# A gated-loop attention with a SwiGLU layer: the norm's sums spread by a tile of ones, and a power on 128 columns

## The chip, the cores and the metric

The kernel runs on one core of one Trainium2 chip. The core has five engines that work side by side, each through its own list of instructions in order: TensorE (PE in the profile, with its weight loads as PEld), VectorE (DVE), ScalarE (ACT), GpSimd (POOL) and SyncE (SP, which only issues DMA transfers here). The metric is the device time of one execution in microseconds, the median of several runs. Everything is in fp32. SBUF is the on-chip memory, PSUM the memory that PE writes its products to, in eight banks.

## What is computed

Cut to its core, the reference is this:

```python
# attention: batch 4, heads 8, 768 steps, head size 48
mag = np.sqrt(a_re**2 + a_im**2)
scale = np.minimum(mag, 0.999) / (mag + 1e-6)
for t in range(S):                       # S_re, S_im: (B, H, 48, 48)
    S = (a_t * scale_t) * S + k_t v_t^T  # complex gate, row by row
    y[:, :, t] = q_t @ S.real
x = y.transpose(0, 2, 1, 3).reshape(3072, 384)
# feed-forward: 384 -> 1536 -> 384
rms = np.sqrt(np.mean(x * x, axis=-1, keepdims=True) + 1e-6)
xn = x / rms * rms_g
g = xn @ w_gate
out = (g / (1 + np.exp(-g)) * (xn @ w_val)) @ w_out
```

The change touches the line of `rms` and the division by it.

## The kernel before

**Tiles.** The 3072 tokens are 24 chunks of 128 (C = 128), six to a batch. A chunk's attention output stands transposed in PSUM, `yT`: 128 features on the partitions, 3 blocks of features (ND = 3) by 128 tokens along the columns. So a token is a column, and its sum of squares runs over the partitions and the three blocks.

**Stages.** For each chunk `attend(n)` makes the masked scores, the output `yT` and the next state; its last part, with the stage name "norm", makes the normalized `xT`. Two chunks are a group (`GROUPS`, L670), and after the second of them `feed(g, xT)` multiplies the group's 256 columns of `xT` with the gate and value weights (groups `bank<-xT,wg` and `bank<-xT,wv` in the profile), takes silu and product into `hT`, and multiplies with `wo`; from the third group on (`split`) the last product is done with seven half products and sums on DVE (tiles `mid`, `ot`, `S` views of `hT`). Ahead of the chunks, `gates(u)` works on the complex gates of one or two chunks (tiles `t`, `in`, `turns`, `kin`, `rot`), on ACT and DVE, and moves `rot` to `kq` by DMA.

**The norm, step by step (L1123 to L1149).**
1. ACT squares `yT` into `sq`; DVE multiplies `yT` by the weights `gcol` into `yg` and adds the three blocks of `sq` into the first. For the first four chunks (`LIGHT` units) ACT makes `yg` instead and PE adds the blocks.
2. PE: `sq` is loaded as weights and multiplied with the single column `ones` (L1136, group `bank<-ones,sq`). The result is one column, `col`: a token's sum on each partition.
3. DVE (L1138, helper `ts`): times 1/384, plus 1e-6, into the chunk's column of `ssv`, a tile that keeps these values of all 24 chunks.
4. POOL (L1139): that column to the power -0.5, in `rs`, with a tile `mhalf` of -0.5 as exponent. There are two `rs` tiles, used in turn.
5. PE (L1142, group `bank<-ident,rs`): `rs`, its one column read 128 times, is loaded as weights and multiplied with the identity. The result `wide` has each token's factor on all partitions, along the columns.
6. DVE (L1149, helper `tt`): `yg` times `wide`, spread over the three blocks, into the group's `xT`. `yg` stands in SBUF, `wide` in PSUM.

Both products and `wide` and `col` use bank 7, which the transposes of `kt` use as well. There is one `sq` tile and two of `yg` and `rs`.

**The guard.** At the end the kernel compares kept values with limits in a tile `ok` (L1269 on), adds up the outcomes, and runs a general version if one is out of bounds; it does not run here. One comparison is that `ssv` is at least twice 1e-6.

**What sets the order.** Every operation is recorded by `Flow.add` (L519) with its engine, a cost given by hand, and what it reads and writes; `Flow.schedule` (L550) then plays the list through with these costs and takes, on each engine, of the operations that are ready the one with the earliest due time, worked backwards from the products of the feed. `Flow.issue` (L645) writes the instructions down in that order. So the order is fixed when the kernel is built, by costs and not by what happens on the chip; every instruction's line in the profile is L648, and the groups are told apart by their tiles. A changed cost or operation can move all instructions behind it. DMA transfers are issued on SP in this order too (up to eight outstanding in the planner's account), the weights' on POOL.

Of the kernel before, what the change touches and what calls it, by code (L numbers as in the profile page):

```python
# [14 lines left out]
ALU = mybir.AluOpType  # L15
# [3 lines left out]
P = 128  # L19
C = 128  # L20
# [3 lines left out]
EPS_RMS = 1e-6  # L24
# [437 lines left out]
class Flow:  # L462
# [56 lines left out]
    def add(self, eng, calls, dur, reads=(), writes=(), table=None, land=None, due=None, after=(), behind=()):  # L519
        op = dict(i=len(self.ops), eng=eng, calls=calls, dur=dur, deps=set(), table=table, land=land,  # L520
                  base=due, stage=self.stage, behind={o["i"] for o in behind})
        self.ops.append(op)
        op["deps"].update(o["i"] for o in after)
        for ap in reads:
            self.note(op, ap, False)
        for ap in writes:
            self.note(op, ap, True)
        return op
# [122 lines left out]
def fast(tc, ctx, qT, kT, v, a_re, a_im, w_gate, w_val, w_out, rms_g, out, H, bad):  # L651
# [27 lines left out]
    def room(name, shape, dtype=FP32):  # L679
        t = mem.tile(shape, dtype, name=name, tag=name)  # L680
        row = 1
        for x in shape[1:]:
            row *= x
        rooms[t.tensor.name] = (name, row * mybir.dt.size(dtype))
        keep.append(t)
        return t
# [25 lines left out]
    def tt(o, x, y, op=ALU.mult, eng="DVE", **kw):  # L712
        e = nc.vector if eng == "DVE" else nc.gpsimd
        dur = 0.15 + 1.04e-3 * cols(o) if eng == "DVE" else 0.25 + 2.2e-3 * cols(o)
        return add(eng, [(e.tensor_tensor, (), dict(out=o, in0=x, in1=y, op=op))], dur, [x, y], [o], **kw)
# [7 lines left out]
    def ts(o, x, c1, c2, op0, op1=None, **kw):  # L723
        k = dict(op1=op1) if op1 is not None else {}
        return add("DVE", [(nc.vector.tensor_scalar, (),
                            dict(out=o, in0=x, scalar1=c1, scalar2=c2, op0=op0, **k))],
                   0.15 + 0.52e-3 * cols(o), aps(x, c1, c2), [o], **kw)
# [51 lines left out]
    def mms(list_, dur, **kw):  # L779
        calls, reads, writes = [], [], []  # L780
        for o, l, r, start, stop in list_:
            calls.append((nc.tensor.matmul, (o,), dict(lhsT=l, rhs=r, start=start, stop=stop)))
            reads += [l, r]
            writes.append(o)
        return add("PE", calls, dur, reads, writes, **kw)

    def mm_time(n, m=P):
        return 2 * max(0.84e-3 * n, 0.83e-3 * m)
# [6 lines left out]
    ident = room("ident", [P, P])  # L795
    causal = room("causal", [C, C])
    mhalf = room("mhalf", [P, 1])
    ones = room("ones", [P, 1])
    halfpi = room("halfpi", [P, 1])
    mid = room("mid", [P, 1])  # L800
# [26 lines left out]
    states = [room(f"state{i}", [D2, NP, 2, 80]) for i in range(2)]  # L827
    sqs = [room(f"sq{i}", [P, ND, C]) for i in range(1)]
    ygs = [room(f"yg{i}", [P, ND, C]) for i in range(2)]
    ssv = room("ssv", [P, N])  # L830
    rss = [room(f"rs{i}", [P, 1]) for i in range(2)]
    sgs = [room(f"sg{i}", [P, 512]) for i in range(2)]
    ots = [room(f"ot{i}", [C, DM]) for i in range(2)]
    sums = room("sums", [P, 2, HD * DH])
# [6 lines left out]
    fill(warm, 1.0, due=-300.0)  # L841
    act(warm, warm, AF.Abs_reciprocal_sqrt, due=-300.0)
    for t, x in ((ones, 1.0), (halfpi, PI / 2), (mid, -(RE_MAX + RE_MIN) / 2),
                 (width, -(RE_MAX - RE_MIN) / 2), (mhalf, -0.5), (zeros, 0.0)):
        fill(t, x)
    for t in ves + states:
        fill(t[:, :, :, D:], 0.0)
# [221 lines left out]
    def attend(n):  # L1069
        flow.stage = "attend", n  # L1070
        ve, am, kq = ves[n % 3], ams[n % 2], kqs[n % 2]
        vv = ve[:, :, :, 0:D].rearrange("t m e d -> t (m e) d")
        dma(vv, v[n * C:(n + 1) * C, :].rearrange("t (h d) -> t h d", d=D), behind=moved[min(n - 1, HOLD)] if n else ())
        k, q = kq[:, :, 0:C], kq[:, :, C:2 * C]
        for a in range(2):
            ps = banks[4 + a]
            s = ps.rearrange("s (h t) -> s h t", h=HH)
            mms([(s[:, h], k[:, a * HH + h], q[:, a * HH + h], True, True) for h in range(HH)],
                HH * mm_time(C), due=EARLY.get(n))
            tt(am[:, a * HH:(a + 1) * HH], s, causal.unsqueeze(1).to_broadcast([C, HH, C]))  # L1080
        first, last = n % NCH == 0, n % NCH == NCH - 1
        prev, new = states[(n + 1) % 2], states[n % 2]
        ps = banks[6]
        yT = ps[:, 0:DM].rearrange("p (j t) -> p j t", j=ND)
        lines = [[] for _ in range(4)]
        vf, sf = (x.rearrange("p m e d -> p m (e d)") for x in (ve, prev))
        for i in range(4 * ND):
            j, c = divmod(i, 4)
            m, r = divmod(i, 3)
            o = yT[c * BLK:(c + 1) * BLK, j]  # L1090
            part = [(2 * m, 0)] if r == 0 else [(2 * m, 1), (2 * m + 1, 2)] if r == 1 else [(2 * m + 1, 3)]
            todo = []
            for h, g in part:
                todo.append((vf[:, m, g * BLK:(g + 1) * BLK], am[:, h]))
                if not first:
                    todo.append((sf[:, m, g * BLK:(g + 1) * BLK], q[:, h]))
            for x, (l_, r_) in enumerate(todo):
                lines[c].append((o, l_, r_, x == 0, x == len(todo) - 1))
        order = [lines[c][i] for i in range(len(lines[0])) for c in range(4)]
        mms(order, len(order) * mm_time(C) / 4 * 1.1 + 0.15)  # L1100
        if not last:
            kt = kts[0]
            for a in range(2):
                ps = banks[7 - 3 * a]
                kp = ps[:, 0:HH * D2].rearrange("t (h d) -> t h d", h=HH)
                calls = [(nc.tensor.transpose, (kp[:, h], k[:, a * HH + h], ident[0:D2, 0:D2]), {})
                         for h in range(HH)]
                add("PE", calls, HH * 0.085, [k[:, a * HH:(a + 1) * HH], ident], [kp])
                act(kt[:, a * HH:(a + 1) * HH], kp, AF.Copy)
            ps = banks[5][0:D2, 0:DM]  # L1110
            st = ps.rearrange("p (h d) -> p h d", h=H)
            mms([(st[:, h], kt[:, h], vv[:, h], True, True) for h in range(H)], H * mm_time(D, D2))
            st4 = ps.rearrange("p (m e d) -> p m e d", m=NP, e=2)
            u, i = unit_of[n], n - UNITS[unit_of[n]][0]
            decay = decays[way_of(u)][:, :, i].rearrange("p (m e) -> p m e", e=2).unsqueeze(3).to_broadcast([D2, NP, 2, D])
            new4 = new[:, :, :, 0:D]
            if first:
                tt(new4, st4, decay)
            else:
                tt(new4, st4, prev[:, :, :, 0:D], ALU.add)  # L1120
                tt(new4, new4, decay)

        flow.stage = "norm", n  # L1123
        sq, yg = sqs[0], ygs[n % 2]
        act(sq, yT, AF.Square)
        if unit_of[n] in LIGHT:
            for j in range(ND):
                act(yg[:, j], yT[:, j], AF.Copy, scale=gcol[:, j:j + 1])
        else:
            tt(yg, yT, gcol.unsqueeze(2).to_broadcast([P, ND, C]))  # L1130
            tt(sq[:, 0], sq[:, 0], sq[:, 1], ALU.add)
            tt(sq[:, 0], sq[:, 0], sq[:, 2], ALU.add)
        ps = banks[7]
        col = ps[:, C:C + 1]
        parts = range(ND if unit_of[n] in LIGHT else 1)
        mms([(col, sq[:, j], ones, j == 0, j == parts[-1]) for j in parts], 0.25 * len(parts))  # L1136
        sv = ssv[:, n:n + 1]
        ts(sv, col, 1.0 / DM, EPS_RMS, ALU.mult, ALU.add)  # L1138
        add("POOL", [(nc.gpsimd.tensor_tensor, (), dict(out=rss[n % 2], in0=sv, in1=mhalf,  # L1139
                                                        op=ALU.pow))], 0.9, [sv, mhalf], [rss[n % 2]])  # L1140
        wide = ps[:, 0:C]
        mms([(wide, rss[n % 2].to_broadcast([P, P]), ident, True, True)], 0.25)  # L1142
        g = group_of[n]
        ns = GROUPS[g]
        x, lo = xplace[g]
        wide_ = len(ns) * C
        xT = xTs[x][:, lo:lo + ND * wide_].rearrange("p (j t) -> p j t", j=ND)
        i = n - ns[0]
        tt(xT[:, :, i * C:(i + 1) * C], yg, wide.unsqueeze(1).to_broadcast([P, ND, C]))  # L1149
        return xT  # L1150

    xplace = {g: (g % 3, 0) for g in range(len(GROUPS))}
# [113 lines left out]

    ne = N * ND
    NW = len(looks)
    ok = room("ok", [P, 2 * ne + NU + 2 * NW + N])  # L1269
    okc = room("okc", [P, 1])  # L1270
    ef = ends.rearrange("p j n -> p (j n)")
    o = 0
    for in_, limit, op in ((ef, P_MIN, ALU.is_ge), (ef, 1.0, ALU.is_le), (range_, 0.0, ALU.is_le),
                           (small, 1.25 * 2.0 ** -15, ALU.is_ge), (large, 2.0, ALU.is_lt),
                           (ssv, 2.0 * EPS_RMS, ALU.is_ge)):
        w_ = in_.shape[1]
        ts(ok[:, o:o + w_], in_, limit, None, op)
        o += w_
# [62 lines left out]
```

## Time and profile before

| what | us |
|---|---|
| median of 3 runs | 740.79 (740.71 to 741.93) |
| the profiled execution's own time | 740.29 |
| its span, first to last instruction | 738.6 |
| DVE products `xT<-yg,bank`, 24 in all | 13.1 |
| DVE sums `sq<-sq`, 40 in all | 11.4 |
| PE products `bank<-xT,wg` and `bank<-xT,wv` | 201.0 and 198.4 |

The granted TensorE clock of the execution is 0.987 of full speed. The page gives, for each engine, how long it was busy and what ended its idle time; the chain of work that ended last says which engine's time is the kernel's time. A fp32 product is two instructions on PE, so 24 products are a group of 48. PE's instructions overlap, so what one costs is read from the distance between starts (those of weight loads, PEld, are the clearest), not from its length.

How the guard's and the queues' parts stand in the profile: `ok<-ssv` is one DVE instruction of 179 ns on 128x24, and DMA issues appear on the line SPq of the timeline with the time for which the queue was taken.

### The profile page before, as it was taken

The numbers are of one execution on the slowest core, as the hardware profiler recorded it, in microseconds if no ns is written. First come the engines' busy times: TensorE is split into PE (matmuls) and PEld (weight loads), VectorE is DVE, ScalarE is ACT, GpSimd is POOL, SyncE is SP. The second block draws the span as 40 slices with busy tenths as digits, with TensorE's granted clock in tenths as the row PEclk, the third lists the DMA queues.
The fourth block names the chain that finished last, engine by engine and source line by source line (L and its number), as shares of the span: only waits on it lengthen the run. The fifth ranks groups of instructions, "written<-read, shape, count | busy, mean of one in ns | idle before, by whom it ended". The sixth has DMA issues, their size and how long they took to land.

```text
span 738.6 us, 12320 instructions
## 1 busy us (share of the span) xinstructions
PE 694.7 (94%) x5050; PEld 623.9 (84%) x5050; DVE 470.6 (64%) x738; ACT 332.1 (45%) x450; POOL 39.4 (5%) x71
## 2 busy tenths in 40 slices
PE   0369999999999999999999999999999999999996
PEld 0368877877899899899899899899899899899885
DVE  5989987779987977967646546656834234233121
ACT  8567656937576925813915623722821110110010
POOL 3132100000000000000000000000000000000000
PEclk9968999999999999999999999999999999999999
DMA  8697565536455355535222202314111102200000
GB/s 298 209 294 235 161 154 166 163 82 169 127 138 149 99 154 150 181 106 146 70 65 66 75 12 73 95 27 119 54 40 30 51 12 55 65 1 2 22 0 27
DMA packets 100144, 76.47 MB, mean 104 GB/s; under 512 B 40944, under 2 KB 90864, under 8 KB 100080
## 3 DMA queue, kind: packets, MB, share of 16 engines
q1 hardware_dynamic: 96016, 61.05, 30.3%
q0 software_dynamic: 3264, 14.16, 5.3%
q8 instruction: 42, 0.69, 0.4%
q10 hardware_dynamic: 800, 0.39, 0.2%
q14 instruction: 22, 0.18, 0.1%
HBM read 51.91 MB, written 4.72 MB: 77 GB/s over the span
## 4 chain that ended last, share of the span: by engine, by line
PE 92%; DVE 4%; ACT 1%; POOL 1%; issue 1%; DMA 1%; DVEq 0%; POOLq 0%; ACTq 0%
PE bank L648 92%; DVE wg L648 1%; DVE turns L648 1%; DVE wv L648 1%; DMA in<-in_a_re_dram 1%; ACT t L648 0%; DVE t L648 0%; DVE rot L648 0%; ACT L648 0%; DVE in L648 0%; POOL rs L648 0%; DVE xT L648 0%; ACT turns L648 0%; DVE am L648 0%; ACT wo L648 0%
## 5 line engine op out<-in xcount | busy, mean ns | idle before, releaser
L648 PE MATMUL bank<-xT,wg 128*128 128x256 f32 x864 | 201.0, 383 | 1.9 <-DVE xT L648 1.9
L648 PE MATMUL bank<-xT,wv 128*128 128x256 f32 x864 | 198.4, 379 | 0.0
L648 PEld LDWEIGHTS bank<-xT,wg 128*128 128x128 f32 x864 | 164.8, 192 | 25.1 <-DVE xT L648 2.6
L648 PEld LDWEIGHTS bank<-xT,wv 128*128 128x128 f32 x864 | 163.5, 190 | 22.2
L648 DVE TENSOR_TENSOR hT<-bank,sg 128x512 f32<-128x512 f32 x72 | 49.6, 689 | 120.9 <-PE bank L648 114.9
L648 PE MATMUL bank<-wo,hT 128*128 128x192 f32 (+1 forms) x576 | 123.4, 357 | 0.4 <-DVE hT L648 0.4
L648 PEld LDWEIGHTS bank<-wo,hT 128*128 128x128 f32 x576 | 94.4, 190 | 11.8 <-issue 1.4
L648 ACT ACTIVATE sg<-bank 128x512 f32<-128x512 f32 x72 | 43.0, 597 | 130.4 <-PE bank L648 127.4
L648 ACT ACT_TABLE_LOAD x67 | 86.0, 1283 | 7.3 <-DVE rot L648 4.7
L648 PE MATMUL bank<-kq 96*128 96x128 f32 x384 | 52.3, 290 | 28.2 <-DMA kq<-rot 28.2
L648 PEld LDWEIGHTS bank<-kq 96*128 96x128 f32 x384 | 49.5, 203 | 29.8 <-issue 29.0
L648 ACT ACTIVATE sq<-bank 128x384 f32<-128x384 f32 x24 | 11.8, 491 | 106.7 <-PE bank L648 106.6
L648 DVE TENSOR_TENSOR rot<-kin,turns 128x768 f32<-128x768 f32 x48 | 44.6, 952 | 14.6 <-DMA kq<-rot 14.4
L648 POOL TENSOR_TENSOR rs<-ssv,mhalf 128x1 f32<-128x1 f32 x24 | 19.4, 810 | 586.6 <-DVE ssv L648 498.0
L648 ACT ACTIVATE kt<-bank 128x384 f32<-128x384 f32 x40 | 18.5, 489 | 66.0 <-PE bank L648 65.9
L648 PE MATMUL bank<-sums,hT 128*128 128x192 f32 x240 | 45.1, 329 | 0.0
L648 PEld LDWEIGHTS bank<-sums,hT 128*128 128x128 f32 x240 | 39.4, 190 | 0.0
L648 DVE TENSOR_TENSOR hT<-hT 128x768 f32<-128x768 f32 x40 | 38.2, 955 | 0.9
L648 PE MATMUL bank<-am,ve 128*32 128x128 f32 x768 | 37.8, 281 | 0.0
L648 ACT ACTIVATE turns<-in 128x768 f32<-128x768 f32 (+1 forms) x39 | 29.9, 789 | 17.1 <-DVE rot L648 8.0
L648 DVE TENSOR_TENSOR am<-bank,causal 128x512 f32<-128x512 f32 x48 | 32.7, 686 | 7.1 <-PE bank L648 6.5
L648 ACT ACTIVATE t<-t 128x768 f32<-128x768 f32 (+1 forms) x39 | 30.9, 792 | 7.9 <-DVE t L648 7.2
(108 smaller groups left out, 729.0 us busy)
## 6 DMA issues: line engine op xcount, KB each, us to landing
kq<-rot SPq DMA_DIRECT2D x144, 128.0 KB, 2.4
ve<-in_v_dram SPq DMA_DIRECT2D x24, 192.0 KB, 3.1
kin<-in_q_dram SPq DMA_DIRECT2D x24, 192.0 KB, 2.7
kin<-in_k_dram SPq DMA_DIRECT2D x24, 192.0 KB, 4.1
wo<-in_w_gate_dram SPq DMA_DIRECT2D x6, 768.0 KB, 5.7
out_dram<-ot SPq DMA_DIRECT2D x24, 192.0 KB, 2.2
wo<-in_w_val_dram SPq DMA_DIRECT2D x6, 768.0 KB, 4.3
wo<-in_w_out_dram SPq DMA_DIRECT2D x6, 768.0 KB, 4.3
```

Of the source, the lines that this page charges most:

```text
L648: fn(*args, **kw)
```

## The change

The first product takes a tile of ones, 128x128, as weights and `sq` as the moving side: its result has each token's sum on all partitions, along 128 columns. Scaling (DVE) and power (POOL) are done on 128x128 values instead of 128x1, in place in `rs`, which is 128 columns wide now. The second product is gone, and the product into `xT` reads `rs` in SBUF. `ssv` is gone; instead a DMA puts the first row of `rs` into row n of a tile `most`, filled with ones at the start, and the guard compares `most` with the limit's power. The planner's cost of the power is 1.5 us instead of 0.9; the cost of a product is `mm_time(C)` instead of 0.25. The tile named `mean` is filled with ones; the factor 1/384 stays in the scaling.

```diff
+    mean = room("mean", [P, P])
+    most = room("most", [P, C])
...
-    ssv = room("ssv", [P, N])
-    rss = [room(f"rs{i}", [P, 1]) for i in range(2)]
+    rss = [room(f"rs{i}", [P, C]) for i in range(2)]
...
-                 (width, -(RE_MAX - RE_MIN) / 2), (mhalf, -0.5), (zeros, 0.0)):
+                 (width, -(RE_MAX - RE_MIN) / 2), (mhalf, -0.5), (zeros, 0.0), (mean, 1.0), (most, 1.0)):
...
-        col = ps[:, C:C + 1]
+        wide = ps[:, 0:C]
         parts = range(ND if unit_of[n] in LIGHT else 1)
-        mms([(col, sq[:, j], ones, j == 0, j == parts[-1]) for j in parts], 0.25 * len(parts))
-        sv = ssv[:, n:n + 1]
-        ts(sv, col, 1.0 / DM, EPS_RMS, ALU.mult, ALU.add)
-        add("POOL", [(nc.gpsimd.tensor_tensor, (), dict(out=rss[n % 2], in0=sv, in1=mhalf,
-                                                        op=ALU.pow))], 0.9, [sv, mhalf], [rss[n % 2]])
-        wide = ps[:, 0:C]
-        mms([(wide, rss[n % 2].to_broadcast([P, P]), ident, True, True)], 0.25)
+        mms([(wide, mean, sq[:, j], j == 0, j == parts[-1]) for j in parts], mm_time(C) * len(parts))
+        rs = rss[n % 2]
+        ts(rs, wide, 1.0 / DM, EPS_RMS, ALU.mult, ALU.add)
+        add("POOL", [(nc.gpsimd.tensor_tensor, (), dict(out=rs, in0=rs, in1=mhalf.to_broadcast([P, C]), op=ALU.pow))],
+            1.5, [rs, mhalf], [rs])
+        dma(most[n:n + 1, :], rs[0:1, :])
...
-        tt(xT[:, :, i * C:(i + 1) * C], yg, wide.unsqueeze(1).to_broadcast([P, ND, C]))
+        tt(xT[:, :, i * C:(i + 1) * C], yg, rs.unsqueeze(1).to_broadcast([P, ND, C]))
...
-    ok = room("ok", [P, 2 * ne + NU + 2 * NW + N])
+    ok = room("ok", [P, 2 * ne + NU + 2 * NW + C])
...
-                           (ssv, 2.0 * EPS_RMS, ALU.is_ge)):
+                           (most, (2.0 * EPS_RMS) ** -0.5, ALU.is_le)):
```

## The prediction

> **What bounds the kernel now.** I read the head of the page first: how busy each engine is and who holds the chain of work that ended last.
>
> ```profile
> span 738.6 us, 12320 instructions
> ...
> PE 694.7 (94%) x5050; PEld 623.9 (84%) x5050; DVE 470.6 (64%) x738; ACT 332.1 (45%) x450; POOL 39.4 (5%) x71
> ...
> PE 92%; DVE 4%; ACT 1%; POOL 1%; issue 1%; DMA 1%; DVEq 0%; POOLq 0%; ACTq 0%
> ```
>
> TensorE (PE) holds 92% of the chain, so time that PE loses is time lost. The table of windows, asked for the stretch in which the chain is one run of PE, says whether it has any slack (columns: length, then busy time of PE, PEld, DVE, ACT, POOL, then clock, DMA share and rate):
>
> ```profile
> 117.10:685.00 567.90, 567.90 (x4228) 515.37 (x4228) 359.89 (x579) 249.98 (x327) 14.43 (x20) 1.00 0.32 87
> ```
>
> PE is busy for all of its 567.90 us there. What is taken off PE is a gain; what makes PE wait is a loss; DVE (360 of 568) and POOL (14) have room, so their work counts only where PE waits for its outcome. The groups that the change touches, with shapes kept apart:
>
> ```profile
> L648 POOL TENSOR_TENSOR rs<-ssv,mhalf 128x1 f32<-128x1 f32 x24 | 19.4, 810 | 586.6 <-DVE ssv L648 498.0 <-DVE ends L648 88.6
> ...
> L648 DVE TENSOR_TENSOR xT<-yg,bank 128x384 f32<-128x384 f32 x24 | 13.1, 547 | 6.5 <-PE bank L648 6.5
> ...
> L648 PE MATMUL bank<-ident,rs 128*128 128x128 f32 x48 | 9.9, 289 | 1.8 <-POOL rs L648 1.8
> L648 PE MATMUL bank<-ones,sq 128*128 128x1 f32 x64 | 9.3, 232 | 3.5 <-ACT sq L648 2.9 <-ACT kt L648 0.6
> ...
> L648 DVE TENSOR_SCALAR ssv<-bank 128x1 f32<-128x1 f32 x24 | 3.7, 154 | 9.5 <-PE bank L648 9.5
> ...
> masks.py:199 POOL TENSOR_SCALAR_AFFINE_SELECT ident<-ident 128x128 f32<-128x128 f32 x1 | 0.3, 294 | 0.1
> ```
>
> The power is 24 instructions on one column, and its mean of 810 ns hides two values. Here it is in two places of the timeline (start, length, engine): the first beside a DVE product of two tiles, the second, at 506 us, with DVE idle.
>
> ```profile
> 343.58 0.16 DVE L648 TENSOR_SCALAR ssv<-bank 128x1 f32<-128x1 f32 x1 [0.90 <-PE bank L648]
> 343.65 0.95 DVE L648 TENSOR_TENSOR t<-t,t 128x768 f32<-128x768 f32 x1
> 343.82 1.19 POOL L648 TENSOR_TENSOR rs<-ssv,mhalf 128x1 f32<-128x1 f32 x1 [6.81 <-DVE ssv L648]
> ```
>
> ```profile
> 506.12 0.55 POOL L648 TENSOR_TENSOR rs<-ssv,mhalf 128x1 f32<-128x1 f32 x1 [50.12 <-DVE ssv L648]
> ```
>
> With DVE's product running (it ends at 344.60) the power ends at 345.01, that is 0.41 us after it, and takes 1.19; with DVE idle it takes 0.55. So a power cannot read while DVE reads two tiles of SBUF; of its 0.55, about 0.14 is dispatch and 0.41 the column.
>
> **What the change takes off.** PE loses the 24 second products (48 instructions). One costs PE the distance to the next weight load. The first product of a chunk has the same price, read here: its two loads start at 505.41 and the next at 505.68.
>
> ```profile
> 505.41 0.35 PEld L648 LDWEIGHTS bank<-ones,sq 128*128 128x128 f32 x2
> ...
> 505.68 0.95 PEld L648 LDWEIGHTS bank<-hT 128*128 128x128 f32 x6
> ```
>
> For the second product the same distance is 0.27 (loads at 449.04, next 449.31): 24 x 0.27 = 6.5 us off PE. The first product keeps two weight loads and now streams 128 columns instead of one; scores of 128 columns cost 0.12 per instruction (16 weight loads of bank<-kq in 1.92 us), so 0.24 to 0.27 either way: nothing. Also gone are one hop to PE and back per chunk.
>
> **What it adds off PE.** The scaling reads 128 columns of PSUM: 0.154 for one, 0.198 for 72 (ok<-ends), so about 0.2; it lies under PE work. Two fills of 128x128 on POOL (0.2 each) lie in the first 20 us, where POOL waits anyway. 24 rows go out by DMA on SP's queue, each behind its power. The page's list of issues counts 258 on SP, at 0.60 each (the one of ve at 344.48) 155 us of the 738.6, so 24 more (14 us) find room; but a row waits on SP for its power, and with it wait the kq transfers queued behind, by as much as the power is late, for PE's next scores. Those scores come after the feed that waits for the same power, so I take nothing, and up to 5 us for the range. The product xT now reads rs from SBUF where it read PSUM: same 0.547, but it becomes a product of two SBUF tiles.
>
> **The price that the trace does not show** is X, the power on 128 columns. From below: POOL's one row that reads many columns is the select on 128, (294 - 100)/127 = 1.5 ns a column (100 ns is its 128x1 fill), so X = 0.55 + 127 x 1.5 ns = 0.74 us. From above: columns that overlap in nothing, 0.14 + 128 x 0.41 = 53 us. Between ends this far apart: the one-column power takes 0.35 more than the one-column copy (0.20, seen<-kq), so there is much arithmetic behind it, some dozens of dependent steps where the select has one or two; ten to fifteen times the select's rate is 15 to 22 ns. I take 19 ns: X = 0.55 + 2.4 = 3.0 us, as an estimate, with 2 to 5 as its own spread.
>
> A page speaks for less. The Trainium skill, GPSIMD Engine Reference, "Elementwise — side-by-side cycle accounting", has about 2.6 cycles a column for a two-input operation (an addition): an estimate of 0.83 us for X, and with it the sum would be 738.6 - 6.5 = 732 us of span. No run shows it for a power.
>
> **What X does to PE.** The order of the instructions is fixed when the kernel is built. In the new order nine of twelve pairs look like chunks 14 and 15. From the start of the even chunk's product to the next feed's first product PE has seven blocks of three 192-column products (0.965 each: 12 loads in 1.93), two blocks of four transposes (0.42, from 453.30 to 453.72) and the two norm products (0.25): 8.1 us of cover; the odd product starts at 3.6. DVE has, in order: scaling even; rot 0.95, two sq sums 0.28, mid 0.35, hT 0.95, mid 0.35 (together 3.2); scaling odd; xT even 0.55; mid, two ends; xT odd 0.55. Each stands behind the one before.
> From the start of the even product: result 0.4, scaling 0.2, hop 0.1, so its power starts at 0.7.
> (a) If a power does not hold DVE up, scaling odd ends at 4.2, the odd power at 4.3 + X, and xT is ready 0.7 later: 5.0 + X against 8.1. Up to X = 3.1 it costs nothing; past 3.4 the two powers queue on POOL and the loss is 2X - 6.7 a pair.
> (b) If it holds DVE's two-tile products until it is done, rot waits until 0.7 + X, scaling odd ends at 4.1 + X, xT even takes 0.55, the odd power X again, hop and xT odd 0.65: 5.3 + 2X. The loss is 2X - 2.8 a pair: at X = 3, 3.2.
> Which? The rows above show that POOL waits for DVE. The other way round the trace has one column's worth:
>
> ```profile
> 113.72 1.94 DVE L648 SCALAR_TENSOR_TENSOR t<-t,t 128x768 f32<-128x768 f32 x2
> 113.89 1.19 POOL L648 TENSOR_TENSOR rs<-ssv,mhalf 128x1 f32<-128x1 f32 x1 [10.70 <-DVE ssv L648]
> ```
>
> Two products in 1.94, where the two rot at 233.34 take 1.83: the second was held up by 0.11 while the power read its column. With 128 columns the reading lasts as long as the power, so I take (b); (a) is the lower end. The last three pairs have little of the gate work on DVE, 1.5 instead of 3.2 between, so 2X - 4.5 there, 1.5 each at X = 3.
>
> The first pair lies in the fill, where the power of chunk 1 is on the chain today with 2.05 us (51.79) and the second product behind it; X = 3 for the one and nothing for the other is even, and the weight transfers that POOL issues behind it come 1 us later, before a feed that is far off.
>
> The Trainium skill says it outright and against this change: SBUF — State Buffer, "Who interferes with whom", has the port pair of VectorE and GpSimd as a lock held for a whole instruction, and a Vector instruction with two SBUF inputs contends for it. The trace agrees in one direction (1.19 against 0.55) and has 0.11 us in the other. By the page the sum is that of (b), 768; without it, that of (a), 734.
>
> **Sum.** 738.6 - 6.5 + 9 x 3.2 + 3 x 1.5 = 765.4 us of span. The profiled execution took 740.29, 1.7 more than its span; the median of the runs is 740.79, 2.2 more. So 768 us. With X = 2 it is 738.6 - 6.5 + 9 x 1.2 + 2.2 = 745; with X = 5, 738.6 - 6.5 + 9 x 7.2 + 3 x 5.5 + 2.2 = 816. The likeliest case's own range is 742 to 816. The stalls eat the whole gain at 9 x (2X - 2.8) = 6.5, X = 1.76.
>
> **Rivals.**
> - The power is cheap, X up to 1.7. For it: the select's 1.5 ns a column would make it 0.74, one hop less, and PE without slack, so that 6.5 us come off whole: 738.6 - 6.5 + 2.2 = 734; at X = 1.7, 9 x 0.6 more, 740. Against: 0.35 us of arithmetic in one column. This is the side that is not slower. Chance 0.24.
> - The power overlaps its columns badly, X from 5 to 12. Then PE waits at every pair, 24 us more for each us of X, under (a) too: at X = 8 under (b) 738.6 - 6.5 + 9 x 13.2 + 3 x 11.5 + 2.2 = 888. For it: dozens of steps at more than one a cycle are a lot to ask of a loop. Against: nothing but the select's rate. Chance 0.20.
> - Columns hardly overlap, X from 12 to 53. POOL, busy 39 us now, becomes the bound: at X = 20, 738.6 - 6.5 + 9 x 37.2 + 3 x 35.5 + 2.2 = 1176. For it: 0.41 us for one column, and no row with a second. Chance 0.15.
>
> **How the numbers follow.** The forecast (X from 1.7 to 5) has 0.41. Faster by over 0.2%, about what a measurement of this kernel can tell from no change (1.5 us), is the cheap rival less its upper edge: 0.20. Within 0.2% are that edge and 0.01 of the forecast: 0.05. Slower is the rest: 0.75. The range leaves out 0.08 below 735 (the whole gain) and 0.12 above 1050 (X over 15).
>
> **What would show it.** The group of POOL's power with 128x128: a mean near 3 us (under 1.7 the cheap rival, over 5 the others). PE waiting before bank<-xT,wg on DVE xT, 1 to 4 us in nearly every group, where it now waits 1.9 us in all. DVE's rot, hT or sq starting when a power ends, at lengths as before: (b); starting under it: (a). The products of mean and sq at 0.24 to 0.27 per chunk, and no ident,rs. The prediction is wrong if the power takes under 1.7 us or over 5, or if PE waits mostly before other work than the feed.

## The result, and the profile after

The changed kernel takes 1192.74 us, the median of 4 runs (1191.60 to 1195.53), beside 740.96 for the kernel before: 1.610 times as long, with a 95% interval of 1.607 to 1.613. The profiled execution took 1191.60, with a span of 1189.8.

The head of its page, with the same three lines that were shown of the kernel before, and the two groups that carry the news:

```profile
span 1189.8 us, 12328 instructions
...
PE 726.9 (61%) x5002; PEld 645.0 (54%) x5002; DVE 477.3 (40%) x738; ACT 332.2 (28%) x450; POOL 522.6 (44%) x73
...
issue 63%; POOL 26%; PE 4%; DVE 3%; ACT 2%; DMA 1%; POOLq 0%; DVEq 0%; ACTq 0%
...
L648 POOL TENSOR_TENSOR rs<-rs,mhalf 128x128 f32<-128x128 f32 x24 | 499.2, 20809 | 556.2 <-DVE rs L648 555.5
...
L648 DVE TENSOR_TENSOR xT<-yg,rs 128x384 f32<-128x384 f32 x24 | 14.9, 621 | 445.4 <-POOL rs L648 445.4
```

One power takes 20.8 us instead of 0.8. DVE's product into xT waited 445.4 us for it, 24 times. No engine is full any more: POOL, the slowest link, works 44% of the span, and PE has fallen from 94% to 61%. That is how a wait looks, as opposed to a new bound. The chain, in which PE had 92%, does not help here: for 63% of the span it finds nothing that was waited for ("issue"). The list of PE's own waits says where the time stood (engine and tile, whom it waited for, us in total, times, the longest):

```profile
PE bank L648 <- DVE xT L648: 183.2, 6, 35.3
PE bank L648 <- DVE ot L648: 173.4, 6, 35.6
PE bank L648 <- DVE mid L648: 34.5, 2, 17.3
PE bank L648 <- DMA kq<-rot: 29.2, 2, 28.3
PE bank L648 <- ACT sq L648: 17.3, 2, 15.5
PE bank L648 <- ACT kt L648: 15.4, 2, 14.2
```

The same list of the kernel before begins so:

```profile
PE bank L648 <- DMA kq<-rot: 28.2, 1, 28.2
PE bank L648 <- ACT sq L648: 2.9, 1, 2.9
PE bank L648 <- DVE xT L648: 1.9, 3, 0.9
```

The wait for the first kq transfer was there before. The others are new, or were under 3 us. DVE's `ot` and `mid` take 0.55 and 0.35 us, so they are not the cause: they stand on DVE behind an xT that waits for a power, and the wait is put down to the instruction that came last. The waits for ACT (15.5 and 14.2 us) stand in the first two pairs; in the first, ACT had stood still for 16.3 us behind a step of the weights on POOL, which came after the power in POOL's list. One pair of chunks in the timeline, 14 and 15 (start, length, engine, what it waited for):

```profile
432.93 41.40 POOL L648 TENSOR_TENSOR rs<-rs,mhalf 128x128 f32<-128x128 f32 x2 [52.84 <-DVE rs L648]
...
434.25 0.96 DVE L648 TENSOR_TENSOR rot<-kin,turns 128x768 f32<-128x768 f32 x1
...
435.39 0.95 DVE L648 TENSOR_TENSOR hT<-hT 128x768 f32<-128x768 f32 x1
...
453.68 0.75 DVE L648 TENSOR_TENSOR xT<-yg,rs 128x384 f32<-128x384 f32 x1 [16.88 <-POOL rs L648]
...
474.37 0.56 DVE L648 TENSOR_TENSOR xT<-yg,rs 128x384 f32<-128x384 f32 x1 [19.52 <-POOL rs L648]
...
474.98 5.49 PE L648 MATMUL bank<-xT,wv 128*128 128x256 f32 x12 [34.42 <-DVE xT L648]
```

Three things stand there. The two powers lie end to end on POOL, 41.4 us. DVE's products of two SBUF tiles (rot, hT) run beside the power at their usual 0.95 us. And PE, after 34.4 us of waiting, needs 5.49 us for twelve instructions that take 2.75 in the kernel before:

```profile
233.64 2.75 PE L648 MATMUL bank<-xT,wv 128*128 128x256 f32 x12
```

The windows around that place say why (length, busy time of PE, PEld, DVE, ACT, POOL, then the granted clock, DMA share, rate):

```profile
440.50:474.90 34.40, 0.06 (x1) 0.00 (x0) 1.70 (x6) 2.12 (x2) 33.83 (x2) 0.54 0.18 46
474.90:478.90 4.00, 3.92 (x9) 3.20 (x10) 4.00 (x7) 1.78 (x2) 0.00 (x0) 0.50 0.27 98
478.90:482.90 4.00, 4.00 (x16) 3.30 (x15) 3.90 (x10) 2.13 (x2) 0.00 (x0) 0.77 0.81 264
482.90:500.00 17.10, 17.10 (x81) 15.06 (x80) 14.00 (x17) 14.11 (x18) 0.00 (x0) 1.00 0.39 113
```

After the wait PE has half its clock for about four microseconds, part of it for some more, and then all. It had lost the clock within the wait: 0.80 over the first 4.5 us (440.5 to 445), 0.50 from then on.

So the 451.2 us by which the span grew (1189.8 - 738.6) have two parts, read from the two lines of busy time. PE's idle time went from 738.6 - 694.7 = 43.9 to 1189.8 - 726.9 = 462.9 us, 419.0 more. Its busy time went from 694.7 to 726.9, 32.2 more, with 48 instructions fewer.

### The profile page after: what moved, and what is told of

Its sections match the earlier page's. It is cut to its first block, busy times and chain, and to the rows that moved or that the text cites. A ratio compares the mean times of both kernels' runs of the same rounds, so it can differ in the third digit from the quotient of the medians.

```text
span 1189.8 us, 12328 instructions
## 1 busy us (share of the span) xinstructions
PE 726.9 (61%) x5002; PEld 645.0 (54%) x5002; DVE 477.3 (40%) x738; ACT 332.2 (28%) x450; POOL 522.6 (44%) x73
## 4 chain that ended last, share of the span: by engine, by line
issue 63%; POOL 26%; PE 4%; DVE 3%; ACT 2%; DMA 1%; POOLq 0%; DVEq 0%; ACTq 0%
POOL rs L648 26%; PE bank L648 4%; DVE turns L648 1%; DMA hT<-in_w_out_dram 1%; ACT t L648 0%; DVE wv L648 0%; POOL junk L648 0%; ACT L648 0%; ACT turns L648 0%; DVE t L648 0%; ACT wo L648 0%; DMA in<-in_a_re_dram 0%; DVE wo L648 0%; DVE wg L648 0%; DVE rot L648 0%
## 5 line engine op out<-in xcount | busy, mean ns | idle before, releaser
L648 POOL TENSOR_TENSOR rs<-rs,mhalf 128x128 f32<-128x128 f32 x24 | 499.2, 20809 | 556.2 <-DVE rs L648 555.5
L648 PE MATMUL bank<-xT,wg 128*128 128x256 f32 x864 | 217.9, 406 | 253.0 <-DVE ot L648 173.4
L648 PEld LDWEIGHTS bank<-xT,wg 128*128 128x128 f32 x864 | 176.6, 206 | 282.9 <-DVE ot L648 175.2
L648 PE MATMUL bank<-xT,wv 128*128 128x256 f32 x864 | 205.8, 389 | 104.3 <-DVE xT L648 103.6
L648 PEld LDWEIGHTS bank<-xT,wv 128*128 128x128 f32 x864 | 168.2, 196 | 129.6 <-DVE xT L648 104.5
L648 DVE TENSOR_TENSOR xT<-yg,rs 128x384 f32<-128x384 f32 x24 | 14.9, 621 | 445.4 <-POOL rs L648 445.4
L648 PEld LDWEIGHTS bank<-wo,hT 128*128 128x128 f32 x576 | 97.2, 193 | 14.0 <-issue 1.8
L648 PE MATMUL bank<-sums,hT 128*128 128x192 f32 x240 | 48.1, 347 | 34.5 <-DVE mid L648 34.5
L648 PEld LDWEIGHTS bank<-sums,hT 128*128 128x128 f32 x240 | 43.2, 204 | 35.1 <-DVE mid L648 35.1
L648 ACT ACTIVATE t<-in 128x768 f32<-128x768 f32 (+1 forms) x26 | 20.3, 790 | 107.1 <-DVE ends L648 85.5
```

The costliest lines, as they stand in the source:

```text
L648: fn(*args, **kw)
```

## The experiments

The theory after the result: the loss is the power's arithmetic, some 160 ns for each of 128 columns, with PE bare under it; the rest of the change is worth what was forecast for a cheap power, and the clock takes a few microseconds after each wait. The rivals: the new order, the rows that go out by DMA, the exponent's form, or POOL as the bound.

**A product in the power's place** (the output is not normalized):

```diff
-        add("POOL", [(nc.gpsimd.tensor_tensor, (), dict(out=rs, in0=rs, in1=mhalf.to_broadcast([P, C]), op=ALU.pow))],
+        add("POOL", [(nc.gpsimd.tensor_tensor, (), dict(out=rs, in0=rs, in1=mhalf.to_broadcast([P, C]), op=ALU.mult))],
```

> The power is replaced by a product with the same two operands and the same cost in the plan, so the output is not normalized; every engine's order stays that of the changed kernel. Theory (the loss is the power's arithmetic, some 160 ns for each of its 128 columns): POOL's instruction takes under 1.2 us, PE waits for no feed, and with 24 second products gone the time is 733 to 738 us. Rival (the new order, the rows that go out by DMA, or xT reading SBUF cost by themselves): 745 us or more, with PE still waiting before the feed.

Measured: 737.74 us against 740.60, ratio 0.9958 (0.9942 to 0.9975). POOL's group, from the list with shapes apart, and the head of the page:

```profile
PE 689.7 (94%) x5002; PEld 619.3 (84%) x5002; DVE 475.8 (65%) x738; ACT 331.6 (45%) x450; POOL 36.4 (5%) x73
...
L648 POOL TENSOR_TENSOR rs<-rs,mhalf 128x128 f32<-128x128 f32 x24 | 13.7, 571 | 586.2 <-DVE rs L648 585.5 <-DVE ends L648 0.7
```

The same instruction with another operation takes 0.57 us in the mean, 0.40 where DVE leaves it alone (at 450.32). With it the change gains 2.9 us of the median. So, with a short operation there, nothing else in the change costs anything that counts: not the order, not the DMA rows, not xT's second tile in SBUF. PE's busy time is 5.0 us shorter, 6.5 had been counted; in the same execution PE waits 3.2 us more (736.8 - 689.7 = 47.1 of idle time against 43.9), most of it in the fill, for xT of the first pair.

**The power on half of the columns** (the other half of the tokens get no power):

```diff
-        add("POOL", [(nc.gpsimd.tensor_tensor, (), dict(out=rs, in0=rs, in1=mhalf.to_broadcast([P, C]), op=ALU.pow))],
+        add("POOL", [(nc.gpsimd.tensor_tensor, (), dict(out=rs[:, 0:64], in0=rs[:, 0:64], in1=mhalf.to_broadcast([P, 64]), op=ALU.pow))],
```

> The power is taken of the first 64 of the 128 columns alone; half of the tokens are scaled wrongly. Theory (a price per column): 0.55 + 63 x 0.159 = 10.6 us for the power; a pair waits 2 x 10.6 - 6.7 = 14.5 us instead of 34.7, 12 pairs, and some 35 us stay for PE's slow clock after each wait: 935 to 960 us. Rival (a fixed price of a wide form, such as leaving a fast path): the power stays near 20 us and the time near 1190.

Measured: 950.61 us, and this group:

```profile
L648 POOL TENSOR_TENSOR rs<-rs,mhalf 128x64 f32<-128x64 f32 x24 | 255.2, 10645 | 559.0 <-DVE rs L648 555.8 <-issue 2.4 <-DVE ends L648 0.8
```

One column 0.55, 64 columns 10.6, 128 columns 20.8: (10.645 - 0.551)/63 = 160 ns and (20.809 - 10.645)/64 = 159 ns a column. The price is one of columns, with no step between these three points, and the kernel's time follows it.

**The exponent from a full tile**: the tile of the first product is filled with -0.5 and serves as exponent; the scaling takes -2/384.

```diff
-        add("POOL", [(nc.gpsimd.tensor_tensor, (), dict(out=rs, in0=rs, in1=mhalf.to_broadcast([P, C]), op=ALU.pow))],
+        add("POOL", [(nc.gpsimd.tensor_tensor, (), dict(out=rs, in0=rs, in1=mean, op=ALU.pow))],
...
-        ts(rs, wide, 1.0 / DM, EPS_RMS, ALU.mult, ALU.add)
+        ts(rs, wide, -2.0 / DM, EPS_RMS, ALU.mult, ALU.add)
```

> The exponent is read from a full tile of 128 columns of -0.5 (the tile of the first product, which is filled with -0.5 instead of 1, the scaling taking -2/384) instead of one column read 128 times. Theory (arithmetic per column): the power stays at 20.7 us and the time within 1% of 1192.7. Rival (the exponent's repeated reading makes it slow): the power falls to a few us and the time below 850.

Measured: 1195.08 us, the power 20.9 us in the mean. Reading one column over and over is not the cause.

**Without the rows for the guard:**

```diff
-        dma(most[n:n + 1, :], rs[0:1, :])
```

> The DMA of a row of rs into the guard's tile is left out (the guard then sees ones). Theory: rows wait on SP for a power that PE waits for anyway, so 1180 to 1195 us. Rival (transfers of kq held up behind the rows on SP start the next scores late): 1150 us or less.

Measured: 1192.40 us. The rows cost nothing here.

**The power alone, in the kernel before**: it reads the one column 128 times, the second product stays.

```diff
-        add("POOL", [(nc.gpsimd.tensor_tensor, (), dict(out=rss[n % 2], in0=sv, in1=mhalf,
+        add("POOL", [(nc.gpsimd.tensor_tensor, (), dict(out=rss[n % 2], in0=sv.to_broadcast([P, C]),
+                                                        in1=mhalf.to_broadcast([P, C]),
...
-        mms([(wide, rss[n % 2].to_broadcast([P, P]), ident, True, True)], 0.25)
+        mms([(wide, rss[n % 2][:, 0:1].to_broadcast([P, P]), ident, True, True)], 0.25)
```

> The kernel before, with nothing changed but the width of the power: it reads the chunk's one column 128 times and writes 128 equal columns, and the second product reads the first of them. Theory (the power's width alone makes the loss): 20.7 us a power; in the trace of before PE takes up the second product 1.9 us after the even power's start and 1.4 after the odd one's, so 12 x (18.8 + 19.3) = 457 us of waits and 20 to 50 us of slow clock: 1210 to 1250 us. Rival (the first product's new form, the scaling of 128 columns or the missing second product have a part in it): below 1100.

Measured: 1243.50 us. From the list of PE's waits:

```profile
PE bank L648 <- POOL rs L648: 447.1, 24, 21.2
```

With nothing of the change but the power's width the loss is there, larger than in the change itself, because here PE meets each of the 24 powers on its own and not two at a time. PE's busy time is 754.5, 59.8 over the kernel before at the same instructions: 24 waits and 24 slow starts.

**The true cost in the plan:**

```diff
-            1.5, [rs, mhalf], [rs])
+            20.8, [rs, mhalf], [rs])
```

> The changed kernel, with one number of the plan altered: the power's cost is 20.8 us instead of 1.5, so the order of all engines is planned anew around its true length. Theory (the loss is not POOL's work, 24 x 20.7 = 497 us beside a PE that needs 735, but that the order leaves 8 us of PE work over a wait of 42): with other work put over it most of the wait goes, and the time is 745 to 850 us. Rival (POOL or the two tiles of rs and yg are the bound whatever the order): 1050 us or more.

Measured: 772.45 us, ratio 1.043 (1.041 to 1.045), with the same 24 powers. Its groups and waits:

```profile
L648 DVE TENSOR_TENSOR xT<-yg,rs 128x384 f32<-128x384 f32 x24 | 15.1, 628 | 11.5 <-POOL rs L648 11.4
```

```profile
PE bank L648 <- DMA kq<-rot: 58.6, 2, 30.3
...
PE bank L648 <- DVE xT L648: 6.3, 3, 5.5
```

501 us of power have all but vanished behind PE's work; DVE waits 11.4 us for them instead of 445.4. So POOL was not the bound: the order gave a 42 us chain 8 us of cover, since the plan knew 1.5 us where there were 20.8. What is left is one wait of 30.3 us in the fill, in which PE waits for the second pair's kq while the first two powers run and the first feed stands behind them, and 5.5 us at the end.

**The true cost, and the first and last two chunks on ACT**, with the reciprocal root that ACT has instead of scaling and power (eps is a tile of 1e-6):

```diff
+        if n in (0, 1, 22, 23):
+            act(rs, wide, AF.Abs_reciprocal_sqrt, scale=1.0 / DM, bias=eps)
+        else:
...
+                20.8, [rs, mhalf], [rs])
```

> The changed kernel with the power's true cost in the plan (20.8), and the reciprocal root on ACT instead of scaling and power for chunks 0, 1, 22 and 23, where nothing is left to cover a power: in the fill POOL also issues the weights' transfers, at the end there is no other work. Theory (with the true cost in the plan only the fill, 30 us, and the end, 6 us, were lost): 735 to 745 us. Rival (the power's 20.7 us hold up more than the planner sees): 755 us or more.

Measured: 755.08 us, ratio 1.019 (1.017 to 1.022). The expectation missed by 10 us, and the result stands at the lower edge of the rival's: the powers hold up more than those two places. The wait of 30 us is gone, but PE's busy time is 696.4, 6.7 more than in the kernel with a product in the power's place, and its idle time is 9.7 more (753.2 - 696.4 = 56.8 against 47.1). Nearly all of the new idle time lies before 147 us: 3.4 us for DVE's hT at 83 us, 4.7 instead of 0.6 for a transfer of kq at 129, and for xT 5.4 instead of 3.5 and 1.9 instead of 1.1. What stands behind each of these was not followed further.

**ACT's root for all chunks:**

```diff
-        ts(rs, wide, 1.0 / DM, EPS_RMS, ALU.mult, ALU.add)
-        add("POOL", [(nc.gpsimd.tensor_tensor, (), dict(out=rs, in0=rs, in1=mhalf.to_broadcast([P, C]), op=ALU.pow))],
-            1.5, [rs, mhalf], [rs])
+        act(rs, wide, AF.Abs_reciprocal_sqrt, scale=1.0 / DM, bias=eps)
```

> POOL's power and DVE's scaling are replaced by one reciprocal root on ACT, read from PSUM with 1/384 as scale and 1e-6 as bias; the spread sums stay. Theory (the power alone is what costs; without it the change is worth what the kernel with a product in its place showed, 737.7): 732 to 742 us, with up to 16 more table loads of 1.28 us on ACT, which is busy less than half of the span. Rival (a table load ahead of the root comes before each feed and PE waits for it): 745 us or more.

Measured: 740.34 us (10 runs, 738.78 to 743.14) against 740.73, ratio 0.9996 (0.9983 to 1.0009): no difference. ACT makes 82 table loads instead of 67, 15 more, and PE waits for ACT's `rs` 1.3 us in all, so the rival is out. PE's busy time is 689.9, as short as with a product, and the span 738.3: what PE saves it waits again. The spread sums are then harmless, but not worth having. No version here beats the kernel before by more than the 0.4% of the kernel with a product, which does not compute the norm.

**PE kept at work during the wait**, with products that nobody uses, first 70 before every feed:

```diff
+        add('PE', [(nc.tensor.matmul, (busy,), dict(lhsT=mean, rhs=wg[:, 0, 0, 0:256],
+            start=True, stop=True))] * 70, 0.1, [mean, wg[:, 0, 0, 0:256]], [busy], due=clock[0] + 1.0)
```

> The changed kernel, with 70 products of 256 columns that nobody uses (some 30 us at full clock) recorded ahead of each feed's first product, into the bank of the norm's sums, so that PE works through most of the wait for the power. Nothing else is added. Theory (some 32 us of the loss are PE's slow clock in the first 4 us after each wait): the waits for xT are as late as before, but the clock is full after them, and in spite of 12 x 30 us of added PE work the time falls by 20 to 40 us, to 1150 to 1175. Rival (the matmuls are slow after a wait for another cause, or the added work delays the feed): 1190 us or more.

Measured: 1252.48 us, a miss. At six pairs PE waits in two pieces, or the idle products themselves had to wait for the bank of the sums: there they began only after a first wait of 14 to 17 us and ran on beyond the end of the second. Counted from feed to feed in the two traces, these six pairs took 9 to 15 us longer each, the other six 5 us less in all. So the test was made again with 77 of them, at seven of the eight groups with one long wait.

> As the run before with products that nobody uses, mended where that one went wrong: 77 of them (33 us), and only ahead of the feeds of groups 2 to 8, the ones at which PE waits 34 to 35 us in one piece. Theory (PE's clock is low after a long wait): seven feeds begin at full clock, 2 to 3 us saved at each, so 1170 to 1183 us although 232 us of PE work are added. Rival (the slow first products have another cause, or the added work is on the path): 1192 us or more.

Measured: 1179.77 us, 13 less than without (the kernel before took 741.09 beside it). Chunks 14 and 15 again, in the timeline:

```profile
437.49 33.40 PE L648 MATMUL bank<-wg,mean 128*128 128x256 f32 x154
...
472.25 2.86 PE L648 MATMUL bank<-xT,wv 128*128 128x256 f32 x12 [1.35 <-DVE xT L648]
```

PE still waits for xT when the idle products end, and the twelve instructions behind it take 2.86 us instead of 5.49; the clock granted from 472.3 to 476.3 us is 1.00, where it was 0.50. 7 x 33 us of added work made the kernel faster. The slow start after a wait is shown to come from the wait itself.

## Why the prediction was wrong

**What bounds the kernel** was right: PE without slack, so that any wait of PE is a loss. That the loss comes in front of the feed, through xT, was right too: 356.6 us of PE's waits (xT and the `ot` behind it) stand there, and 34.5 more before products that need the `mid` behind xT.

**The step that failed is the price X.** The prediction put "ten to fifteen times the select's rate" behind the one-column power and came to 19 ns a column, X = 3.0 us, with 2 to 5 as its own spread. It measured 159 ns a column and 20.8 us, eight times as much a column and seven times as much in all. The trace had the better row, and the text used it only for the upper end: a single column takes 0.41 us of a power's time, where a whole one-column copy takes 0.20. That time was read mostly as a start-up that later columns share; 0.16 of the 0.41 is what each column costs. No row showed how many steps a power has, from which the ten to fifteen times was guessed. The select's 1.5 ns and the measured product (0.40 us for 128 columns) say what it costs to pass columns through POOL, and nothing of the arithmetic on them. The page of the Trainium skill named there (GPSIMD Engine Reference, "Elementwise — side-by-side cycle accounting") prices a two-input addition at about 2.6 cycles a column, an estimate of 0.83 us. The product stayed under that, and the power took 25 times as much.

**Case (b) was wrong, case (a) right.** The prediction took it that the power holds DVE's products of two SBUF tiles until it is done. In the trace rot, hT and the two sums of sq run in the midst of a power at 0.96, 0.95 and 0.61 us (the pair), as in the kernel before. In these rows only an instruction that starts together with one is held, for about 0.2 us: xT of the even chunk takes 0.75 instead of 0.56, and the rot at 528.03, 0.09 us behind a power's start at 527.94, 1.12 instead of 0.95. The 0.11 us that had been read from the one-column power was therefore most of the effect, not one column's share. The other direction was read rightly: a power that starts while such a product runs takes 22.19 and 21.36 us (at 69.37 and 172.55). The Trainium skill, weighed there (SBUF — State Buffer, "Who interferes with whom"), says of DVE's two-port modes that the shared ports are held for the whole instruction, and of a product of two SBUF tiles that it contends with a GpSimd instruction that reads SBUF. For a power these rows show it at the start alone; the measurement decides.

**Formula (a) holds to about a microsecond.** Its loss for two powers end to end, 2X - 6.7, gives 34.7 us at X = 20.72; PE's wait in the eight groups with one long wait measured 33.8 to 35.6. That 12 x 34.7 = 416 stands so near the 419.0 of added idle time is partly luck: the other four pairs do not have the order that the formula describes, and waited 39.7 and 36.3 us (the first two) and 33.5 (twice). At 64 columns it gives 2 x 10.6 - 6.7 = 14.5, and these waits measured 13.6 to 15.4.

**A term was missing**: PE's clock after a wait. Against the kernel with a product in the power's place, which does the same work on PE, busy time is 726.9 - 689.7 = 37 us longer. The two windows behind the wait of chunks 14 and 15 lack 4 x 0.50 + 4 x 0.23 = 2.9 us of clock, which for 12 waits is 35. The rival that named X = 20 (chance 0.15) came to 1176 us, close to the measurement, but through (b)'s formula and without the clock: two errors, of +22 us (441 against 419) and -37, that partly cancelled. Its mechanism, POOL as the bound, was wrong: POOL was busy 44% of the span, and in another order the same powers cost 32 us.

**What was taken off PE** was mis-sized: 6.5 us forecast, 5.0 us measured in busy time and 2.9 in the median, since the first pair's xT came later in the fill. The cheap rival's 734 would have been 738. Why PE's busy time fell by 5.0 and not 6.5 stays open.

**Taken at nothing and found so**: the fills (0.2 us each), the scaling of 128 columns (0.28 us instead of 0.15), the rows on SP, xT's operand in SBUF (0.547 before, 0.547 with a product).

**Two slips in the working** change nothing above. The sum charges twelve pairs, 9 and 3, though the text takes the first pair as even, so it is 3.2 us too high by its own account. And under (a) the two powers begin to queue where 0.7 + X passes 4.3, at X = 3.6 and not 3.4.

## What to carry to other kernels

A power on POOL is priced by its columns, although a product of the same shape is nearly free: for an operation that no row shows in its wide form, ask what one column costs and multiply, unless a row shows that columns overlap. Put the values along the partitions, as the kernel before did with its one column and a second product, and 128 powers take 0.55 us. A plan made with hand-written costs is as good as its worst cost: the same 24 powers made the kernel 61% or 4% slower with 1.5 or 20.8 us in the plan. And a long wait of PE costs more than its length, because PE here started again at half its clock.

## What the runs showed of the hardware

- POOL's power in fp32: 0.55 us for one column of 128 partitions, 10.6 for 64, 20.7 for 128, whether the exponent is one column read again or a full tile; a product of the same 128 columns 0.40.
- DVE's products of two SBUF tiles run at full speed beside a power (rot at 0.96 us), but for some 0.2 us at its start; the power's length does not grow under those that start after it (20.72 us). A power that starts while one runs took 21.36 and 22.19 us.
- After 34 us of waiting PE had 0.50 of its clock for 4 us and 0.77 over the next 4; after 33 us of idle products and a wait of 1.35 us it had all of it, and twelve matmul instructions took 2.86 us, close to the 2.75 of the kernel before.
